# A chunked recurrence with two expert layers on one core: the first steps reordered

## The chip, the cores and the metric

One core of a Trainium2 chip runs one program. The metric is the device time of one execution in microseconds (us), as the median of three runs. TensorE, VectorE, ScalarE, GpSimd and SyncE (SP, which issues most transfers) run beside each other, each in the order of its own instructions.

## What is computed

The reference has three parts, in float32, each feeding the next. For 4 batches, 8 heads, 768 steps and a head dimension of 40:

```python
for t in range(S):
    y[:, :, t] = np.einsum('bhd,bhde->bhe', rt, state)
    Sa = np.einsum('bhde,bhe->bhd', state, at)
    state_decay = state * wt[:, :, None, :] - np.einsum('bhd,bhe->bhde', Sa, bt)
    state = state_decay + np.einsum('bhd,bhe->bhde', vt, kt)
```

The 3072 tokens of 320 numbers that come out pass a dense layer, `g = h * clip(h + 3, 0, 6) / 6` with `h = x @ w_in` (2048 wide) and `g @ w_out`; then a gate picks one of eight experts for each token, with `relu(x @ w1[e]) @ w2[e]`, 1024 wide, times the gate's weight.

## The kernel before

The recurrence is cut into 24 chunks of 32 steps (`C`, `NCH`), four chunks to a window of 128 steps (`SC`) and two chunks to a pair. Within a chunk the steps are solved at once: for each batch and head, N is a strictly lower 32x32 matrix of products between the scaled `a`, `k` and `b` of the chunk, and T its solved form. The path of one pair is: `turned` (TensorE transposes of the scaled rows, line 478, copied by line 483 into Z and KB), `gram_n` (the products L and N in one bank, line 506), `strict` (mask on VectorE, line 512), `keep` (L back into Z, line 517) and `store` (N to DRAM, `Nd`, line 523). `solve` loads N back from DRAM so that each partition holds one matrix (line 565), copies it twice (line 562), does 30 steps of two operations each (lines 574 and 575), and stores T (`Td`, line 583). `loads_t` (line 610) loads a chunk's T block by block into `Tb`, and `usolve` multiplies with it (u, line 649). The first pair is solved on VectorE, all later ones on GpSimd.

Window preparation (`window`, lines 385 to 453) makes decays from `w` by transposes and scans, and their reciprocals (`inv`, line 435). `scale` (line 439) multiplies the rows of `a`, `k` and `b` (`AKB`, tiles ra, rk, rb) with them. The prepared rows of each chunk go to DRAM in `Ed` and `KBd` by the window's function `keep(j)` (lines 441 to 451), and come back chunk by chunk (`loads_kb`, `loads_e`). `AKB` exists once, so a next window's rows may be loaded (`akb_rows`, line 1241: six transfers for one pair, line 358) only when the old ones are kept and transposed.

The code writes the order of every engine by hand (`tc.manual_schedule()`), and a scheduler adds the waits. Functions passed to `later(n, ...)` run n ticks on. Each transfer of SP or ScalarE holds one of eight completion semaphores (DMAHW0 to 7), and one that gets a semaphore already in use waits for it. The start (lines 1138 to 1284) prepares window 0, transposes and multiplies the first pair, starts `work0` (the first solve), and puts into it, at three of its steps (`S0, S1, S2`), the second pair's products with its solve (`next_gram`), and the first right-hand side followed by a burst of warmers (`before_solved`). Warmers are matmuls whose result nobody reads. `put0` stores T. Then the loop over chunks (line 1297) runs `rhs`, `usolve`, `usolve_cols`, `state`, `gram`, `turn_state`, `yout`, `cols_vr` for chunk c, the products of the pair four chunks ahead, the pieces of the next window and, from chunk 2 on, matmuls of the first dense layer (`dense`, `M.emit`, lines 263 and 304), which fill TensorE.

The dense layer's weights come as int64 pairs and are converted on VectorE (lines 116 to 118), split into two parts (lines 89 and 90), and for `w_out` turned on TensorE (line 158) and multiplied with the gate (line 169). There are 14 such units in a queue `wq`: six of `w_in` (three row blocks by two halves of the columns), then eight of `w_out`. `convert` says at which turn of which chunk how many are taken.

The first solve's own tile N0 lies in the buffer Z2, which the third pair needs as its Z; the loop's first chunk allocates it and GpSimd zeroes it (line 1382). `half_inverse(n)` (lines 1278 to 1284) takes the second window's reciprocals for half the heads and scales `rk` and `rb` with them.

## Time and profile before

| what | us |
|---|---|
| median of three runs | 1117.95 (1116.79 to 1120.19) |
| the profiled execution | 1113.57 |
| its span in the trace | 1111.8 |
| TensorE busy, share of the span | 1009.5, 91% |
| VectorE busy | 666.6, 60% |
| ScalarE busy | 650.1, 58% |
| GpSimd busy | 392.3, 35% |

Rows of a timeline have a start and a duration in us, the engine, the line, the operation, the tile written and the tiles read, the shape and a count; in brackets stands the idle time before it and what ended it. PE is TensorE, DVE VectorE, ACT ScalarE, POOL GpSimd; SPq is the issuing of transfers on SP. float32 matmuls stand in the trace as two instructions for one in the program.

### The profile page before, as it was taken

The numbers are of one execution on the slowest core, as the hardware profiler recorded it, in microseconds if no ns is written. First come the engines' busy times: TensorE is split into PE (matmuls) and PEld (weight loads), VectorE is DVE, ScalarE is ACT, GpSimd is POOL, SyncE is SP. The second block draws the span as 40 slices with busy tenths as digits, with TensorE's granted clock in tenths as the row PEclk, the third lists the DMA queues.
The fourth block names the chain that finished last, engine by engine and source line by source line (L and its number), as shares of the span: only waits on it lengthen the run. The fifth ranks groups of instructions, "written<-read, shape, count | busy, mean of one in ns | idle before, by whom it ended". The sixth has DMA issues, their size and how long they took to land. (4 is left out here: it accounts for less than half of the span.)

```text
span 1111.8 us, 36869 instructions
## 1 busy us (share of the span) xinstructions
PE 1009.5 (91%) x15540; PEld 944.4 (85%) x15540; DVE 666.6 (60%) x1338; ACT 650.1 (58%) x1370; POOL 392.3 (35%) x849
## 2 busy tenths in 40 slices
PE   4757799999999999998998999999999879999995
PEld 4756688888888888887887889999999779999995
DVE  7575447756546546543344455566557797787770
ACT  5324565777788778876677663433333545666551
POOL 5308345084575655846355401000000112332221
PEclk9578686999999999998998999999999989999998
DMA  9694966998798988989447532323333566766630
GB/s 135 126 151 73 165 128 104 128 183 137 135 175 141 159 141 156 159 139 192 95 93 144 111 90 78 100 82 97 104 106 112 191 186 208 220 208 197 209 90 16
DMA packets 362104, 151.82 MB, mean 137 GB/s; under 512 B 318663, under 2 KB 344775, under 8 KB 361932
## 3 DMA queue, kind: packets, MB, share of 16 engines
q1 hardware_dynamic: 352492, 129.45, 57.5%
q0 software_dynamic: 4992, 18.96, 6.0%
q8 instruction: 124, 2.03, 0.9%
q10 hardware_dynamic: 4448, 0.98, 0.5%
q14 instruction: 48, 0.39, 0.1%
HBM read 109.23 MB, written 40.12 MB: 134 GB/s over the span
## 5 line engine op out<-in xcount | busy, mean ns | idle before, releaser
L275 DVE SCALAR_TENSOR_TENSOR gf<-rl,h 128x512 f32<-128x512 f32 x96 | 65.6, 684 | 123.4 <-ACT rl L271 121.6
L263 PE MATMUL h<-xT,wi 128*128 128x256 f32 x768 | 119.9, 300 | 0.0
L280 DVE TENSOR_TENSOR gl<-gf,gh 128x512 fp32r<-128x512 f32 x78 | 55.4, 711 | 92.3 <-ACT gh L279 92.0
L271 ACT ACTIVATE rl<-h,half 128x512 f32<-128x512 f32 x96 | 65.9, 686 | 70.8 <-PE h L263 70.3
L263 PEld LDWEIGHTS h<-xT,wi 128*128 128x128 f32 x768 | 101.6, 196 | 3.4
L304 PE MATMUL x<-wo,gh 128*128 128x328 f32 x368 | 96.7, 348 | 0.5 <-ACT gh L279 0.5
L1703 POOL DMA_INDIRECT out_dram<-cyo,sidx x26 | 26.1, 1003 | 152.9 <-ACT cyo L1702 139.3
L279 ACT CAST gh<-gf 128x512 fp32r<-128x512 f32 x78 | 48.4, 620 | 38.4 <-DVE gf L275 37.9
L517 ACT COPY Z<-Ns 32x512 f32<-32x512 f32 x48 | 29.6, 618 | 64.4 <-DVE Ns L512 64.1
L304 PEld LDWEIGHTS x<-wo,gh 128*128 128x128 f32 x368 | 61.5, 197 | 5.0 <-ACT gh L279 0.7
L506 PE MATMUL LN<-Z,KB 104*64 104x32 f32 x1408 | 55.0, 235 | 9.0 <-POOL Z L1382 5.9
L1496 POOL DMA_DIRECT2D xTb<-xTd x10 | 5.4, 545 | 162.2 <-PE h L263 162.2
L506 PEld LDWEIGHTS LN<-Z,KB 104*64 104x64 f32 x1408 | 50.6, 152 | 14.0 <-POOL Z L1382 6.2
L483 ACT COPY KB<-t 40x512 f32<-40x512 f32 x86 | 49.8, 579 | 16.3 <-PE t L478 14.5
L304 PE MATMUL x<-wo,gl 128*128 128x328 f32 x184 | 59.1, 321 | 0.2 <-DVE gl L280 0.2
L717 PE MATMUL g<-YL,UV 104*64 104x32 f32 x1536 | 55.6, 227 | 0.0
L717 PEld LDWEIGHTS g<-YL,UV 104*64 104x64 f32 x1536 | 50.2, 141 | 5.7 <-issue 1.0
L1673 ACT ACTIVATE ghc<-ch 128x512 fp32r<-128x512 f32 x35 | 20.9, 598 | 51.0 <-PE ch L1667 50.0
L435 DVE RECIPROCAL It<-It 128x320 f32<-128x320 f32 (+1 forms) x20 | 50.3, 2531 | 0.1
L1587 POOL DMA_INDIRECT xg<-Xr,gidx x26 | 29.5, 1136 | 55.3 <-DVE sidx L1072 21.3
L724 DVE TENSOR_TENSOR YL<-g,mask 64x512 f32<-64x512 f32 x48 | 32.9, 685 | 20.3 <-PE g L717 19.9
L1096 PE MATMUL warm<-ident 128*128 128x128 f32 x258 | 44.5, 324 | 0.0
(787 smaller groups left out, 3057.1 us busy)
## 6 DMA issues: line engine op xcount, KB each, us to landing
raw<-in_moe_w_dram SPq DMA_DIRECT2D x26, 512.0 KB
raw<-in_moe_w_dram SPq DMA_DIRECT2D x26, 480.0 KB
xTd<-xT SPq DMA_DIRECT2D x12, 768.0 KB
xTb<-xTd POOLq DMA_DIRECT2D x10, 768.0 KB, 6.5
X<-KBd SPq DMA_DIRECT2D x46, 160.0 KB
raw<-in_moe_w_dram SPq DMA_DIRECT2D x13, 320.0 KB
xpd<-xpart SPq DMA_DIRECT2D x12, 328.0 KB
part<-xpd SPq DMA_DIRECT2D x12, 328.0 KB
```

What stands on the lines that cost most here:

```text
L263: nc.tensor.matmul(hp[:, i, :], lhsT=l, rhs=m, start=j == 0, stop=j == len(seq) - 1)
L271: nc.scalar.activation(v["t"], hv, AF.Relu, bias=half, scale=1.0 / 6.0)
L275: nc.vector.scalar_tensor_tensor(out=v["g"], in0=v["t"], scalar=1.0, in1=hv, op0=ALU.min, op1=ALU.mult)
L279: nc.scalar.copy(gh.rearrange("p i t -> p (i t)"), v["g"])
L280: nc.vector.tensor_tensor(out=gl.rearrange("p i t -> p (i t)"), in0=v["g"], in1=gh.rearrange("p i t -> p (i t)"), op=ALU.subtract)
L304: nc.tensor.matmul(st["x"][tt][:, :NX], lhsT=l[:, i, ts], rhs=W.wo[f][:, m, :], start=fp == 0 and i == 0 and j == 0, stop=fp == NFP - 1 an ...
L435: nc.vector.reciprocal(t, t)
L483: copy(dst[64:104, par::2].rearrange("p g b j t -> p g (b j) t"), pb[HP * par:HP * par + D].rearrange("p g b (j t) -> p g (b j) t", j=2))
L506: nc.tensor.matmul(pv[64 * q:64 * q + 64, g, bb, j, :], lhsT=KB[0:104, h, bb, j].rearrange("p x t -> p (x t)"), rhs=zh[0:104, h, bb, j, :] ...
L717: nc.tensor.matmul(pg[64 * q:64 * q + 64, g, bb, :], lhsT=uv[0:104, h, bb].rearrange("p x t -> p (x t)"), rhs=yl[0:104, h, bb, :], start=T ...
L724: nc.vector.tensor_tensor(out=yl[0:64, par::2], in0=pg[q:q + 64], in1=mask[q:q + 64, None, None, :].to_broadcast([64, 4, B, C]), op=ALU.mult)
L1096: nc.tensor.matmul(t[:, 0, 0:128], lhsT=ident, rhs=ident, start=True, stop=True)
```

## The change

- N is stored by matrix: `Nd` has the axis order h, b, j, i, t instead of i, h, b, j, t. A half's store is four transfers of 256 rows of 128 bytes instead of two of 64 rows of 1 KB; the load of a pair's N is two transfers of 64 rows of 4 KB instead of two of 2048 rows of 128 bytes.
- `keep(2)` and `keep(3)` of the first window go to SP instead of ScalarE, behind `akb_rows(0)`, which now follows `keep(1)`. `akb_rows(1)`, the fourth pair's rows, moves from `next_gram` behind u of chunk 0. Two weight loads (`WA.pull(2)`) move behind the loads of T.
- Z2 is allocated and zeroed, by ScalarE, right behind the store and load of T.
- VectorE scales only the third pair's rows (`pr0`); GpSimd scales the fourth pair's (`pr1`) behind yout of chunk 0. The second half of the reciprocals comes in two quarters, behind gram and behind yout of chunk 0.
- The units of the first weights are taken in another order, and by another `convert`.
- `keep_part` keeps one chunk a call over two chunks where it kept two.

```diff
-    Nd = dram.tile([NCH // 2, C, H, B, 2, C], F32, name="Nd")
+    Nd = dram.tile([NCH // 2, H, B, 2, C, C], F32, name="Nd")
...
+            if self.id == 0:
+                units = [units[n] for n in (0, 2, 4, 6, 7, 1, 8, 3, 5, *range(9, 14))]
...
-        def keep(j, eng=nc.sync):
+        def keep(j):
...
                 for par in range(2):
                     q = 64 * par
-                    nc.sync.dma_start(out=Nd[pr, :, 4 * half + par:4 * half + 4:2].rearrange("i g b j t -> i g (b j t)"), in_=Ns[q + 32:q + 64].rearrange("p (g x) -> p g x", g=2))
+                    for g in range(2):
+                        src = Ns[q + 32:q + 64].rearrange("p (g x t) -> p g x t", g=2, t=C)[:, g]
+                        nc.sync.dma_start(out=Nd[pr, 4 * half + 2 * g + par].rearrange("b j i t -> i (b j) t"), in_=src)
...
     keep(0)
     keep(1)
+    akb_rows(0)
+    keep(2)
+    keep(3)
     for i in range(3):
         now(U[2][i])
         now(U[3][i])
-    keep(2, nc.scalar)
-    keep(3, nc.scalar)
     some(4)
     now(wq, 1)
...
     def next_gram(hf):
-        if not hf:
-            akb_rows(0)
         now(U[2 + hf][3])
         flush_stores()
         if hf:
-            WA.pull(2)
-            akb_rows(1)
             solve(1, nc.gpsimd, None, nc.sync)()()
...
     loads_t(0)
+    Z.append(big.tile([128, H, B, 2, C], F32, tag="Z2", name="Z2"))
+    nc.scalar.copy(Z[2][0:64].rearrange("p h b j t -> p (h b j t)").rearrange("p (n x) -> p n x", x=128), zeros[0:64, None, :].to_broadcast([64, 2 * H, 128]))
     loads_e(0)
+    WA.pull(2)
...
-    scale(0, every)
+    scale(0, every, p=pr0)
...
-    def half_inverse(n):
-        hs = slice(n * H // 2, (n + 1) * H // 2)
+    def inverse(n, of):
+        hs = slice(n * H // of, (n + 1) * H // of)
         inv(every, hs)
         for i in range(1, 3):
-            scale(i, every, hs=hs)
-
-    half_inverse(0)
+            scale(i, every, p=pr0, hs=hs)
+
+    inverse(0, 2)
...
-    convert = {(0, 3): 2, (0, 5): 1, (0, 6): 1, (1, 1): 1, (1, 3): 2, (1, 4): 2, (1, 5): 1, (2, 2): 1, (2, 3): 1, (2, 4): 1}
+    convert = {(0, 6): 1, (1, 1): 1, (1, 2): 1, (1, 3): 1, (1, 4): 1, (1, 5): 1, (2, 1): 2, (2, 2): 1, (2, 4): 1, (2, 6): 1, (3, 1): 1, (3, 3): 1, (3, 5): 1}
...
-            Z.append(big.tile([128, H, B, 2, C], F32, tag="Z2", name="Z2"))
-            nc.gpsimd.memset(Z[2][0:64], 0.0)
...
         slot(usolve, c)
         if c == 0:
             loads_t(1)
+            akb_rows(1)
...
         slot(gram, c)
         if c == 0:
-            half_inverse(1)
+            inverse(2, 4)
...
         slot(yout, c)
+        if c == 0:
+            inverse(3, 4)
+            for i in range(3):
+                scale(i, every, nc.gpsimd, pr1)
```

How this moves the instructions stands in the order of each engine. On SP, round the first load of N (tile N_413 before, N_417 after), with the semaphores that it waits for. Before:

```order
L523 DMA Nd<-Ns_407 32x2x256 [waits DMAHW5_49,DVE_49]
L523 DMA Nd<-Ns_407 32x2x256 [waits DMAHW6_49]
L565 DMA N_413<-Nd 64x32x32 [waits DMAHW4_49,DMAHW5_49,DMAHW3_49,DMAHW6_49,DMAHW0_49,DVE_49]
L565 DMA N_413<-Nd 64x32x32 [waits DMAHW2_49]
```

With the change:

```order
L528 DMA Nd<-Ns_409 32x8x32 [waits DMAHW5_49,DVE_49]
L528 DMA Nd<-Ns_409 32x8x32 [waits DMAHW6_49]
L528 DMA Nd<-Ns_409 32x8x32 [waits DMAHW7_49]
L528 DMA Nd<-Ns_409 32x8x32 [waits DMAHW0_49]
L570 DMA N_417<-Nd 64x1024 [waits DMAHW4_49,DMAHW3_49,DMAHW5_49,DMAHW2_49,DMAHW6_49,DMAHW1_49,DMAHW7_49,DMAHW0_49,DVE_49]
L570 DMA N_417<-Nd 64x1024
```

Before, DMAHW0 and DMAHW2 are held by transfers that ScalarE issues; with the change all eight belong to the stores of N themselves.

Further on in SP's queue, from the rows of the next window to the loads of T (Tb). Before:

```order
L358 DMA rb<-in_b_dram 64x16x40 x2
L523 DMA Nd<-Ns_565 32x2x256 x2
L523 DMA Nd<-Ns_612 32x2x256 x2
L107 DMA wraw<-in_moe_w_in_dram 128x1024
L107 DMA wrawrv<-in_moe_w_in_dram 128x1024
L358 DMA ra<-in_a_dram 64x16x40 x2
L358 DMA rk<-in_k_dram 64x16x40 x2
L565 DMA N1None<-Nd 64x32x32 x2
L583 DMA Td<-N_413 1024x1x32 x2
L610 DMA Tb<-Td 32x8x32 x4
```

With the change:

```order
L361 DMA rb<-in_b_dram 64x16x40 x2
L447 DMA Ed<-Em 32x4x320
L452 DMA KBd<-rk 1024x1x40
L452 DMA KBd<-rb 1024x1x40
L528 DMA Nd<-Ns_569 32x8x32 x4
L528 DMA Nd<-Ns_618 32x8x32 x4
L570 DMA N1None<-Nd 64x1024 x2
L588 DMA Td<-N_417 1024x1x32 x2
L615 DMA Tb<-Td 32x8x32 x4
L107 DMA wraw<-in_moe_w_in_dram 64x1024
```

The weight loads and the second group of window rows (six transfers, of which the listing before leaves out the last two, rb) have gone from between the stores of N and the store of T, and two keeps of three transfers stand ahead of the stores (one is shown).

On VectorE, in chunk 0, from the mask of the gram (YL) to the low half of x (XS). Before:

```order
L724 TENSOR_TENSOR YL<-g_1018,mask 64x4x128 x2
L435 RECIPROCAL It_869<-It_869 128x4x160
L439 TENSOR_TENSOR rk<-rk,It_869 128x4x4x40
L439 TENSOR_TENSOR rb<-rb,It_869 128x4x4x40
L90 TENSOR_TENSOR wi_91<-wf_1004,wi_89 128x512
L90 TENSOR_TENSOR wi_92<-wf_1011,wi_90 128x512
L740 TENSOR_TENSOR x_1149<-y_1116,Et_861 128x320
```

With the change:

```order
L729 TENSOR_TENSOR YL<-g_1012,mask 64x4x128 x2
L438 RECIPROCAL It_873<-It_873 128x4x80
L442 TENSOR_TENSOR rk<-rk,It_873 64x4x2x40
L442 TENSOR_TENSOR rb<-rb,It_873 64x4x2x40
L745 TENSOR_TENSOR x_1134<-y_1101,Et_861 128x320
L438 RECIPROCAL It_873<-It_873 128x4x80
L442 TENSOR_TENSOR rk<-rk,It_873 64x4x2x40
L442 TENSOR_TENSOR rb<-rb,It_873 64x4x2x40
L752 TENSOR_TENSOR XS<-x_1134,XS 128x320
```

Two subtractions of the weights have left this place, and half of the reciprocals and products stands behind x. TensorE's list of chunk 0 has warmers of 4, 2 and 2 matmuls less: two ahead of and within the gram (line 717), one behind yout. On GpSimd the memset of Z behind the second solve's store of T is gone, and three products (ra, rk, rb, 64x32x40 each) stand there, ahead of the third solve.

## Rows read from the trace of the kernel before

**Rows 1.** The page: the span.

```profile
span 1111.8 us, 36869 instructions
```

**Rows 2.** Busy time by stretch: stretch, length, PE, PEld, DVE, ACT, POOL, PEclk, DMA, GB/s.

```profile
91.00:125.00 34.00, 24.83 (x457) 22.49 (x453) 15.74 (x20) 17.56 (x38) 26.11 (x56) 0.75 0.61 105
...
169.90:190.40 20.50, 20.50 (x250) 18.53 (x250) 16.32 (x30) 8.30 (x19) 12.40 (x28) 0.51 0.36 78
...
160.20:196.60 36.40, 35.40 (x542) 31.80 (x541) 24.02 (x40) 21.02 (x51) 20.61 (x47) 0.68 0.72 117
196.60:216.70 20.10, 19.06 (x490) 16.95 (x490) 16.10 (x24) 13.89 (x31) 0.00 (x0) 1.00 0.85 119
216.70:650.00 433.30, 411.62 (x9298) 366.32 (x9297) 224.12 (x347) 329.37 (x714) 241.44 (x594) 0.98 0.79 145
```

**Rows 3.** Timeline of VectorE round the first solve: start, duration, what.

```profile
44.49 0.69 DVE L118 SCALAR_TENSOR_TENSOR wf<-wraw,wf 128x512 int32<-128x512 int32 x1
...
53.01 0.19 DVE L574 TENSOR_TENSOR N<-N 128x30 f32<-128x30 f32 x1
...
71.27 0.22 DVE L578 MEMSET N<- 64x16 f32 x2
```

**Rows 4.** Waits of SP, 0 to 130 us: total, times, longest.

```profile
SPq L565 <- DMA Ed<-Em: 6.0, 1, 6.0
```

**Rows 5.** Timeline of SP's issuing: start, duration, transfers.

```profile
33.26 4.12 SPq L523 DMA_DIRECT2D Nd<-Ns  x4
44.30 2.92 SPq L565 DMA_DIRECT2D N<-Nd  x2
...
77.04 3.60 SPq L565 DMA_DIRECT2D N1None<-Nd  x2
80.74 2.82 SPq L583 DMA_DIRECT2D Td<-N  x2
86.32 1.83 SPq L610 DMA_DIRECT2D Tb<-Td  x4
...
145.64 2.51 SPq L565 DMA_DIRECT2D N2None<-Nd  x2
```

**Rows 6.** Timeline of TensorE: the burst of warmers, u, and grams of later pairs.

```profile
65.58 13.40 PE L1096 MATMUL warm<-ident 128*128 128x128 f32 x96
88.22 0.31 PE L649 MATMUL u<-rh,Tb 128*32 128x40 f32 x2 [9.24 <-DMA Tb<-Td]
...
89.85 1.27 PE L649 MATMUL u<-rh,Tb 128*32 128x40 f32 x58 [0.24 <-DMA Tb<-Td]
...
121.31 3.63 PE L506 MATMUL LN<-Z,KB 104*64 104x32 f32 x64 [5.93 <-POOL Z L1382]
...
206.57 2.04 PE L506 MATMUL LN<-Z,KB 104*64 104x32 f32 x64
```

**Rows 7.** Timeline of VectorE in chunk 0.

```profile
101.83 1.39 DVE L724 TENSOR_TENSOR YL<-g,mask 64x512 f32<-64x512 f32 x2 [12.36 <-PE g L717]
103.25 4.15 DVE L435 RECIPROCAL It<-It 128x640 f32<-128x640 f32 x1
...
110.84 0.49 DVE L740 TENSOR_TENSOR x<-y,Et 128x320 f32<-128x320 f32 x1
```

**Rows 8.** Timeline of GpSimd: a pair of products of the start, the third solve's first copy.

```profile
26.98 3.03 POOL L439 TENSOR_TENSOR ra<-ra,Em 64x640 f32<-64x640 f32 x2
...
150.31 0.60 POOL L562 COPY X2None<-N2None 64x512 f32<-64x512 f32 x1 [29.05 <-DMA N2None<-Nd]
```

**Rows 9.** PE and PEld by stretch: warmers (L1096), then w_out's transposes (L158) and products (L169).

```profile
91.00:125.00 34.00, 11.21 (x59) 9.11 (x59) 0.75 0.61 105
...
126.90:160.20 33.30, 2.75 (x15) 1.88 (x15) 0.91 0.68 138
...
126.90:160.20 33.30, 4.43 (x30) 4.09 (x30) 0.91 0.68 138
```

**Rows 10.** Groups of TensorE, 216 to 650 us: count, busy, mean ns, idle before and releasers.

```profile
L649 PE MATMUL u<-rh,Tb 128*32 128x40 f32 x1216 | 18.6, 214 | 4.9 <-DMA Tb<-Td 3.7 <-ACT rh L641 1.2
```

More of the change, by code (lines that the diff above doesn't have):

```diff
@@ L439, in scale @@
             (eng or nc.vector).tensor_tensor(out=t, in0=t, in1=(v["I"] if i else Em)[p, bs, hs], op=ALU.mult)
-        def keep(j, eng=nc.sync):
+        def keep(j):
             p, c = slice(C * j, C * j + C), SC * sc + j
-            eng.dma_start(out=Ed[c].rearrange("b t f -> t b f"), in_=Em[p].rearrange("p b h e -> p b (h e)"))
+            nc.sync.dma_start(out=Ed[c].rearrange("b t f -> t b f"), in_=Em[p].rearrange("p b h e -> p b (h e)"))
             for x in range(2):
@@ L448, in keep @@
                     continue
-                eng.dma_start(out=KBd[x, C * c:C * c + C].rearrange("t b (h e) -> t (b h) e", e=D), in_=AKB[1 + x][p, :, :, 0:D].rearrange("p b h e -> p (b h) e"))
+                nc.sync.dma_start(out=KBd[x, C * c:C * c + C].rearrange("t b (h e) -> t (b h) e", e=D), in_=AKB[1 + x][p, :, :, 0:D].rearrange("p b h e -> p (b h) e"))
             if j == 0 and sc < NSC - 1:
@@ L549, in solve @@
             tmp = p1.tile([128, 128], F32, tag="tmp", name=f"tmp{pr}{part}")
-        src, dst = Nd[pr].rearrange("i h b j t -> (h b) j i t"), Td[pr].rearrange("(g j) i t -> g j i t", j=2)
+        src, dst = Nd[pr].rearrange("h b j i t -> (h b) j i t"), Td[pr].rearrange("(g j) i t -> g j i t", j=2)
         if part is None:
-            src, dst = Nd[pr].rearrange("i h b j t -> (h b j) i t"), Td[pr]
+            src, dst = Nd[pr].rearrange("h b j i t -> (h b j) i t"), Td[pr]
         else:
@@ L1230, with akb_rows @@
     work0 = solve(0, nc.vector, None, nc.sync)
+    def akb_rows(j):
+        for n in range(6):
+            loads_akb(1, n // 2, j, n % 2)
     keep(0)
     keep(1)
+    akb_rows(0)
+    keep(2)
+    keep(3)
     for i in range(3):
@@ L1235 @@
         now(U[3][i])
-    keep(2, nc.scalar)
-    keep(3, nc.scalar)
     some(4)
     now(wq, 1)
-    def akb_rows(j):
-        for n in range(6):
-            loads_akb(1, n // 2, j, n % 2)
     def next_gram(hf):
-        if not hf:
-            akb_rows(0)
         now(U[2 + hf][3])
@@ L1364, in keep_part @@
         def keep_part(n):
-            if sc == 0 and j == 1:
-                for i in (2 * n, 2 * n + 1):
-                    win[1][-1](i)
+            if sc == 0 and j in (1, 2):
+                win[1][-1](2 * (j - 1) + n)
             elif j < 2 and 0 < sc < NSC - 1:
```

## The prediction

> **What bounds the kernel now.** I read four views, in this order. First the busy time by stretch, against the span [rows 1, 2]. From 216.7 to 650 us TensorE is busy 411.62 of 433.30 us at a clock share of 0.98: that stage is bound by TensorE, and whatever the first 200 us lose is carried whole to the end, because the later stages start from data and not at a time of day. The start is another matter: from 91 to 125 us TensorE is busy 24.83 of 34 us, 11.21 of these with warmers (59 matmuls that compute nothing) [rows 9], and the clock share of 0.75 says that it ran half of that stretch at the lower of its two levels (1.2 GHz, not 2.4). Every edit but the layout of N lies in this start, so the forecast is read from the start's chains.
>
> Second, the timeline of VectorE and the queue of SP round the first solve [rows 3 to 5]. The first solve needs N back from DRAM. The load is issued at 44.30 us although the stores' issue ended at 37.38. SP waited 6.0 us there, for an Ed transfer: one of the six that ScalarE issues for `keep(2)` and `keep(3)`. The order shows why: the load waits for DMAHW0, a completion semaphore that one of these holds. VectorE is through with other work at 45.2 (44.49 + 0.69), gets N only then, and solves from 53.01. The solve ends at 71.5, but the store of T is issued at 80.74: since N, SP has had to issue thirteen transfers of `keep` and `akb_rows(0)`, four stores, two weight loads, six transfers of `akb_rows(1)` and N of the second pair. T is loaded back from 86.32, and the first u ends at 91.1 (89.85 + 1.27) [rows 6].
>
> Third, the chunk that follows [rows 6, 7]. TensorE's gram of the third pair waits 5.93 us for a memset of Z2 on GpSimd, which stands behind the whole second solve, and ends at 124.94. VectorE, after the mask (ends at 103.22), takes a reciprocal of half the heads and four more operations before x at 110.84, for which the transposes on TensorE wait.
>
> Fourth, the wait of the steady stage [rows 10]: from 216 to 650 us u waits 3.7 us in all for T. There the change has little to win and something to lose.
>
> **The change, part by part.** The sum is made against the profiled execution, 1113.57 us with a span of 1111.8. The median of the timed runs, 1117.95, lies 4.4 above it, and I keep that distance.
>
> *First load of N.* With `keep(2)` and `keep(3)` on SP behind the load, nothing of ScalarE's stands ahead of it. Eight stores of 256 rows replace four of 64. Four loads of that very shape (T's, 32x8x32) issue in 1.83 us [rows 5], so the second half's stores, whose data is there at 36.6, are issued by 38.5 and land near 40. The load is then 64 rows of 4 KB a transfer instead of 2048 of 128 B. VectorE is busy until 45.2 anyway, so I put the copies there and the solve at 46.1: 6.9 us earlier, ending at 64.6. Bounds: nothing, if the small stores land as late as today's load is issued, and 6.9, since VectorE's other work is next.
>
> *Store of T and u.* `akb_rows(1)` and two weight loads leave the queue ahead of T; six transfers of `keep` and four stores come in, and N and N1 shrink from 8192 rows to 256. From N's load at 44.30 to T's store at 80.74 about 25,000 small rows passed: twelve window transfers and eight of `keep` at 1024 rows, and N's 4096. That is 690 a us. Six window transfers and eight of `keep` are 14,300, or 21 us: from 42 to 63. The stores and N1's load add about 2, and I take T's issue at 66.5, 2 us behind the solve, where today it is 9.2. From T's issue to the end of u is 10.4 us today with N1's 4096 rows in front; with 128 I take 9. So u ends near 75.5, **15.6 us** earlier with the first term. Bounds: T issued as the solve ends (17.6), or as long after N's load as today, 36.4 us, at 76.4 (5.7).
>
> *Chunk 0.* Today 33.8 us pass from the end of u to the end of the gram. The order takes 8 warmers out, 16 matmuls in the trace at 0.19 us (11.21 over 59), 3.0 us, of which 12, 2.2 us, lie ahead of the mask. Of the reciprocal of half the heads, 4.15, a quarter is half, 2.1, and a product of that width is as wide as x, 0.49 [rows 7]. So, in today's frame: mask ends at 101.0, reciprocal and two products at 104.1, x at 104.6, the second quarter at 107.7, the low half of x at 108.2, its transposes at 108.8, a warmer, then the gram from 109.5 to 111.6, at the 2.04 us that it takes at full clock [rows 6]. Z2's zeros are now a ScalarE copy that waits for T's store alone and lies beside T's way back. That is **13 us**. Bounds: 5.9, if only the memset's wait goes, and 15, if the clock stays up through u as well: the burst of warmers that ends at 78.98, 9 us ahead of u, now ends at its heels.
>
> *Fourth pair.* Its six loads follow u and lie beside chunk 0. Its three products go from VectorE to GpSimd behind the second solve, about 3 us each by a pair of half-width ones of the start [rows 8]. That solve starts with N1, some 16 us earlier, and the third solve waits 29.05 us for its N [rows 8], so they are covered; without that cover the third pair's T would come 9 us later.
>
> *Weights by use.* The conversions stay fourteen, but they move back. A w_out block costs TensorE (2.75 + 4.43)/5 = 1.44 us [rows 9]. Chunk 1 has two fewer: **-3**. Behind u of chunk 3 stand two more, 2.9 on TensorE, and on VectorE some 4.6 (two conversions at 1.3 and the subtractions behind them), which has 16.10 of 20.1 us taken there [rows 2]. Both are then full; I take **+3.5**. Chunk 2's share of VectorE, 24.02 of 36.4 us, has room.
>
> *Stores in the steady stage.* Two more issues a chunk, 0.45 each, stand ahead of the loads of T, against a load of N every second chunk that needs 2.5 us to issue today [rows 5] and then has 64 rows a transfer. I take **+2** (-3 to +8). T's own store is 2048 rows of 128 B; it and N1's 4096 landed within 9.3 us of the first issue, 77.04 to 86.32, so 1024 such rows cost 1.6 us at most.
>
> Here the Trainium skill speaks against the change: *DMA: Bandwidth & Descriptors*, Specifications, gives 512 B as the least transfer at line rate, with a read-modify-write below, and the new stores write 128 B where the old wrote 1 KB. By that rule the last rival below would be the likely one; no row here shows a small write's own duration.
>
> Sum: -15.6 - 13 - 3 + 3.5 + 2 = -26, less 2 for waits that I don't see: 1117.95 - 24 = **1094 us**.
>
> **The rivals.** *The queue stays full.* If T's store comes 36.4 us behind N's load as today, T's term shrinks by 9.9: 1104. For it: six transfers move into this stretch, and the stores double. Against: N's and N1's small rows are gone. *VectorE holds chunks 2 and 3.* The reciprocals of the next window meet eight conversions there instead of three; each chunk could lose 4 us more: 1102. *The clock recovers early.* From 169.9 to 190.4 TensorE runs at the lower level though it is busy throughout [rows 2]; no row shows a cause that the change takes away, so I leave it. If the smoother start keeps the clock up, chunk 2 is bound by VectorE's 24 us plus some 5 of conversions, near 30 and not 36.4: 1088. *Slower: the small stores hold T.* If a half's stores land as late as the 2048 rows of N2's load do (issued at 145.64, copied at 150.31, 4.7 us [rows 5, 8]), T comes some 4 us later in the 20 halves of the steady stage. u waits for T in some chunks already, so if half of that is lost, it is 2 x 20 = 40: 1134. It outweighs the gain from 24/20 = 1.2 us a chunk on. Against it stands T's own store. That an edit doesn't do what it says has little room: the order shows each move.
>
> **The numbers.** Forecast 0.62, queue full 0.13, VectorE full 0.10, clock 0.09, slow stores 0.06. The range, 1081 to 1108, takes in the first four with the bounds of T's term (+10, -2), chunk 0 (+7, -2), the steady stage and the clock. A measurement of this kernel tells about 0.3% (3.4 us) from no change. Faster by more 0.92, within it 0.03 (slow stores near their turning point), slower 0.05.
>
> **What would show it.** Right: N's load issued near 40 and the solve at 46; T's store within 3 us of the solve's end; u ending near 75; no wait of the gram for Z, and the gram's end near 96; w_out blocks fewer in chunk 1 and more in chunk 3; everything from chunk 5 on 22 to 28 us earlier, with chunks as long as today. Wrong: T's store waiting in SP's queue, VectorE without idle time in chunks 2 and 3, or u waiting for T in most chunks.

## The result, and the profile after

| | before | with the change |
|---|---|---|
| median of four runs, us | 1117.37 (1115.79 to 1120.19) | 1129.15 (1128.29 to 1135.16) |
| ratio to before, 95% interval | | 1.012 [1.0086, 1.0155] |
| span of the profiled execution, us | 1111.8 | 1126.8 |
| chunk 0 (u of chunk 0 to u of chunk 1) | 38.7 | 25.1 |
| chunk 1 | 33.4 | 42.9 |
| chunk 2 | 36.4 | 34.6 |
| chunk 3 | 20.1 | 42.2 |
| chunks 5 to 22 | 412.3 | 421.9 |
| u of chunk 23 to the end | 458.8 | 461.9 |

The change makes the kernel 1.2% slower; the forecast was 24 us faster. The lengths are read from the starts of the u rows of each profile, and say where the time went: the first u comes 13.0 us earlier (75.25 for 88.22 in [rows 6]) and chunk 0 gives another 13.6, together 26.5 where 28.6 was forecast. Chunks 1 and 3 then lose 9.5 and 22.1, and the steady stage 9.6.

First the start. Timeline of SP's issuing (start, duration, transfers), to hold against [rows 5]:

```profile
31.41 6.10 SPq L528 DMA_DIRECT2D Nd<-Ns  x8
38.79 1.13 SPq L570 DMA_DIRECT2D N<-Nd  x2
...
59.83 6.13 SPq L528 DMA_DIRECT2D Nd<-Ns  x8
67.40 1.14 SPq L570 DMA_DIRECT2D N1None<-Nd  x2
68.58 1.31 SPq L588 DMA_DIRECT2D Td<-N  x2
73.36 1.94 SPq L615 DMA_DIRECT2D Tb<-Td  x4
```

The wait for Ed is gone and N's load is issued at 38.79, not 44.30. The stores take 6.1 us of issue where they took 4.1 at the same place [rows 5], and the second eight stand ahead of N1 and T. VectorE's timeline, the first and the last row of the solve [rows 3]:

```profile
44.25 1.29 DVE L579 TENSOR_TENSOR N<-N 128x30 f32<-128x30 f32 x1
...
63.62 0.22 DVE L583 MEMSET N<- 64x16 f32 x2
```

The solve ends 7.7 us earlier, T is issued 12.2 us earlier, 4.7 behind the solve and not 9.2. TensorE's timeline, to hold against [rows 6]: u of chunk 0, the gram of the third pair, then in chunk 1 the gate products of a w_out block (8 columns wide) and a half of g, and in chunk 3 a w_out block's transposes:

```profile
75.25 0.31 PE L654 MATMUL u<-rh,Tb 128*32 128x40 f32 x2 [4.66 <-DMA Tb<-Td]
...
97.25 2.06 PE L509 MATMUL LN<-Z,KB 104*64 104x32 f32 x64
...
108.35 0.93 PE L169 MATMUL wg<-wg,wtT 128*128 128x8 f32 x6 [0.64 <-ACT wtT L162]
...
112.02 1.92 PE L722 MATMUL g<-YL,UV 104*64 104x32 f32 x32
...
185.95 0.90 PE L158 MATMUL wt<-ident,wf 128*128 128x128 f32 x3 [6.18 <-DVE wf L118]
```

The gram no longer waits for Z. But half of g takes 1.92 us in chunk 1, and TensorE stands idle for 6.18 us in chunk 3. The same half of g in the kernel before:

```profile
134.93 1.12 PE L717 MATMUL g<-YL,UV 104*64 104x32 f32 x32
```

Busy time by stretch (columns as in [rows 2]): chunks 1, 2 and 3, the steady stage at the length of [rows 2], then two pieces of chunks 1 and 3:

```profile
100.30:143.20 42.90, 40.74 (x562) 36.38 (x561) 24.78 (x36) 21.63 (x51) 21.80 (x31) 0.68 0.66 136
143.20:177.90 34.70, 29.15 (x546) 25.58 (x546) 27.73 (x44) 22.14 (x51) 20.99 (x46) 0.90 0.74 129
177.90:220.00 42.10, 34.76 (x509) 30.68 (x508) 21.89 (x37) 15.90 (x40) 4.30 (x6) 0.59 0.60 93
220.00:653.30 433.30, 405.14 (x9136) 360.47 (x9134) 216.59 (x334) 323.56 (x695) 236.21 (x589) 0.97 0.78 140
...
109.30:133.20 23.90, 23.90 (x267) 21.72 (x265) 12.40 (x19) 7.38 (x19) 4.81 (x2) 0.50 0.52 114
184.40:218.50 34.10, 31.40 (x423) 27.80 (x424) 17.99 (x31) 15.27 (x37) 2.96 (x4) 0.50 0.51 83
```

From 109.3 to 133.2 and from 184.4 to 218.5 the granted clock is 0.50, the lower level (1.2 GHz), though TensorE is busy 23.90 of 23.90 and 31.40 of 34.10 us. Chunk 3 had a share of 1.00 before [rows 2]. So a wait of 0.64 us stands ahead of 24 us at half speed, and one of 6.18 ahead of 34.

Who is late in chunk 3 is read on VectorE and SP, then in chunk 1 on GpSimd and VectorE (timelines):

```profile
177.34 1.10 SPq L107 DMA_DIRECT2D wrawrv<-in_moe_w_out_dram  x1
...
184.51 0.33 DVE L116 TENSOR_SCALAR wf<-wrawrv 128x320 int32<-128x320 int32 x1 [4.22 <-DMA wrawrv<-in_moe_w_out_dram]
...
107.70 3.32 POOL L442 TENSOR_TENSOR rk<-rk,It 64x1280 f32<-64x1280 f32 x1
110.98 3.13 POOL L442 TENSOR_TENSOR rb<-rb,It 64x1280 f32<-64x1280 f32 x1
...
108.31 3.06 DVE L90 TENSOR_TENSOR wo<-wf,wo 128x320 fp32r<-128x320 f32 x1
111.37 2.92 DVE L116 TENSOR_SCALAR wf<-wrawxT 128x320 int32<-128x320 int32 x1
```

The thirteenth weight unit's raw words are asked for at 177.34, behind six transfers of window rows (170.59 to 177.22), and VectorE waits for them until 184.51. In chunk 1 VectorE's operations end just behind GpSimd's products: a subtraction that takes 0.48 us later in the chunk takes 3.06.

The steady stage is told by the u group (TensorE, 220 to 653 us) against [rows 10]: the wait for T grows from 3.7 to 5.9, and the clock share falls from 0.98 to 0.97.

```profile
L654 PE MATMUL u<-rh,Tb 128*32 128x40 f32 x1216 | 19.3, 218 | 7.8 <-DMA Tb<-Td 5.9 <-ACT rh L646 1.7
```

### The profile page after: what moved, and what is told of

It reads as the page before. It is cut to its first block, busy times and chain, and to the rows that moved or that the text cites. A ratio compares the mean times of both kernels' runs of the same rounds, so it can differ in the third digit from the quotient of the medians.

```text
span 1126.8 us, 36918 instructions
## 1 busy us (share of the span) xinstructions
PE 1023.8 (91%) x15528; PEld 955.9 (85%) x15528; DVE 676.5 (60%) x1341; ACT 654.1 (58%) x1371; POOL 398.8 (35%) x851
## 5 line engine op out<-in xcount | busy, mean ns | idle before, releaser
L729 DVE TENSOR_TENSOR YL<-g,mask 64x512 f32<-64x512 f32 x48 | 32.9, 685 | 25.0 <-PE g L722 24.6
```

Of the source, the lines that this page charges most:

```text
L729: nc.vector.tensor_tensor(out=yl[0:64, par::2], in0=pg[q:q + 64], in1=mask[q:q + 64, None, None, :].to_broadcast([64, 4, B, C]), op=ALU.mult)
```

## The experiments

All runs in one table; the ratio is against the kernel before, measured beside each group of runs. Chunk lengths are of one profiled execution each. The same program differs from one execution to the next by up to 25 us in these versions, so small differences between single profiles are not read.

| run | first u | chunk 0 | 1 | 2 | 3 | 5 to 22 | median us (range, runs) | ratio |
|---|---|---|---|---|---|---|---|---|
| e1_raw_first | 77.2 | 24.2 | 42.2 | 35.9 | 30.9 | 421.7 | 1122.3 (1117.7–1129.2, 10) | 1.004 [1.001, 1.007] |
| e2_old_weights | 77.8 | 32.9 | 37.3 | 32.5 | 22.9 | 421.8 | 1115.0 (1109.3–1127.4, 10) | 0.998 [0.994, 1.002] |
| e3_old_nd | 76.1 | 24.1 | 43.0 | 36.6 | 38.9 | 415.2 | 1116.7 (1106.7–1120.3, 10) | 0.996 [0.992, 1.000] |
| e4_vector_scale | 77.1 | 32.6 | 42.6 | 36.4 | 39.8 | 429.0 | 1133.4 (1121.2–1145.7, 10) | 1.011 [1.007, 1.015] |
| e5_swap | 77.4 | 24.5 | 31.9 | 38.1 | 41.0 | 423.3 | 1122.4 (1111.4–1127.9, 10) | 1.002 [0.998, 1.005] |
| e6_start_only | 75.8 | 33.2 | 46.3 | 35.8 | 20.5 | 411.4 | 1108.8 (1104.7–1111.2, 4) | 0.989 [0.984, 0.995] |
| e7_nd_only | 90.2 | 39.2 | 35.4 | 36.6 | 20.1 | 421.3 | 1134.0 (1123.9–1140.5, 10) | 1.013 [1.010, 1.016] |
| e8_combo | 75.3 | 24.3 | 33.4 | 38.5 | 38.8 | 416.2 | 1111.0 (1103.8–1112.4, 8) | 0.991 [0.988, 0.994] |
| e9_products | 76.3 | 33.3 | 37.1 | 36.1 | 20.5 | 411.4 | 1105.3 (1101.6–1106.8, 4) | 0.991 [0.987, 0.994] |
| e10_spread | 75.6 | 23.8 | 35.8 | 45.4 | 21.6 | 413.2 | 1102.1 (1096.4–1102.8, 4) | 0.986 [0.981, 0.990] |
| e11_four_big | 91.0 | 38.8 | 35.1 | 35.7 | 20.5 | 428.8 | 1138.1 (1136.1–1139.8, 4) | 1.019 [1.015, 1.023] |
| e12_t_first | 89.3 | 39.2 | 33.1 | 36.5 | 20.0 | 429.8 | 1136.2 (1134.6–1140.2, 4) | 1.018 [1.014, 1.023] |
| e13_spread_t | 75.6 | 24.6 | 33.0 | 45.5 | 31.4 | 425.1 | 1114.0 (1104.9–1122.3, 12) | 0.996 [0.993, 0.999] |

### The parts undone one at a time

**e1_raw_first**, the changed kernel with one load moved:

```diff
         if c == 2:
+            if pulled[0] < 14 and raws[pulled[0] + 1] <= laid[0]:
+                pulled[0] += 1
+                WA.pull(1)
             for i in range(3):
                 next_akb(i, True)
```

> The changed kernel with one transfer moved: the raw words of the thirteenth weight unit are asked for ahead of the six window rows (ra, rk, rb) of chunk 2, and not behind them. Late weights: in the changed kernel that load was issued at 177.34 us behind six transfers, VectorE waited for it until 184.51, TensorE stood idle for 6.18 us and then ran at the lower clock from 184.4 to 218.5. If that one load is the cause, TensorE has no wait over 1 us in chunk 3, the clock stays up, chunk 3 (u to u) takes 20 to 24 us and not 42.2, and the time is 1107 to 1112 us, that is 17 to 22 below the changed kernel. Rival, the clock: if the stretch at the lower clock would come there anyway, as it came to chunk 2 of the kernel before, only the 6 us of the wait come back: 1122 to 1124. Rival, VectorE full: the wait goes to another conversion, chunk 3 stays over 35 us, 1126 to 1131.

Chunk 3 fell from 42.2 to 30.9 and the 6.18 us of idle time are gone, so that load was the cause of the wait. The time fell by 7 us, into the range of the clock rival, and not by 17 to 22: a wait of 0.81 us is left, for the next unit, with the lower clock behind it (195.4 to 209.1), and another such stretch (171.6 to 185.2) reaches in from chunk 2.

TensorE's timeline in chunk 3 of this run:

```profile
193.89 0.55 PE L158 MATMUL wt<-ident,wf 128*128 128x128 f32 x3 [0.81 <-DVE wf L118]
```

Busy time of its chunk 3 (the clock share is the last number but two):

```profile
179.50:210.30 30.80, 29.50 (x509) 26.38 (x508) 19.82 (x35) 15.79 (x39) 3.67 (x6) 0.69 0.78 117
```

**e2_old_weights**:

```diff
-            if self.id == 0:
-
-                units = [units[n] for n in (0, 2, 4, 6, 7, 1, 8, 3, 5, *range(9, 14))]
...
-    convert = {(0, 6): 1, (1, 1): 1, (1, 2): 1, (1, 3): 1, (1, 4): 1, (1, 5): 1, (2, 1): 2, (2, 2): 1, (2, 4): 1, (2, 6): 1, (3, 1): 1, (3, 3): 1, (3, 5): 1}
+    convert = {(0, 3): 2, (0, 5): 1, (0, 6): 1, (1, 1): 1, (1, 3): 2, (1, 4): 2, (1, 5): 1, (2, 2): 1, (2, 3): 1, (2, 4): 1}
```

> The changed kernel with the order of the weight units and the table of their conversions as before. Late weights: only three conversions are left for chunk 2 and none for chunk 3, so chunk 3 takes some 20 us again (42.2 in the changed kernel), and the 17 us by which u of chunk 2 led are kept from there on, less the 10 that the steady stage loses: 1105 to 1112 us. If the six conversions in chunk 1 meet GpSimd's products there, chunk 1 grows past its 42.9 us, and the time is nearer 1112. Rival, the start itself: if the clock, and not the weights, sets chunks 1 to 3, they last as long as in the changed kernel together (119.7 us), and the time is 1126 to 1132.

Chunk 3 is back at 22.9 and the median 14 us below the changed kernel, 3 us short of what late weights expected; chunk 0 pays, 32.9 for 25.1, as three conversions are back there and TensorE waits 3.99 us behind them, ahead of the gram.

**e3_old_nd**, with the load of N back in the same way:

```diff
-    Nd = dram.tile([NCH // 2, H, B, 2, C, C], F32, name="Nd")
+    Nd = dram.tile([NCH // 2, C, H, B, 2, C], F32, name="Nd")
...
-                    for g in range(2):
-                        src = Ns[q + 32:q + 64].rearrange("p (g x t) -> p g x t", g=2, t=C)[:, g]
-                        nc.sync.dma_start(out=Nd[pr, 4 * half + 2 * g + par].rearrange("b j i t -> i (b j) t"), in_=src)
+                    nc.sync.dma_start(out=Nd[pr, :, 4 * half + par:4 * half + 4:2].rearrange("i g b j t -> i g (b j t)"), in_=Ns[q + 32:q + 64].rearrange("p (g x) -> p g x", g=2))
```

> The changed kernel with N stored as before: two transfers of 64 rows of 1 KB for each half, loaded in rows of 128 bytes. Small stores: from u of chunk 5 to u of chunk 23 the changed kernel takes 421.9 us and the kernel before 412.3; if the four stores of 128-byte rows ahead of T's load cost that, it falls to about 412, and the start gives back 3 to 6 us of its gain by the slower load of N: 1121 to 1125 us. Rival, the order of issue alone: the steady stage keeps its 420 us or more, for another reason (the clock, another transfer ahead of T), and the time is 1129 to 1135.

The steady stage fell from 421.9 to 415.2 and the time by 12 us, more than expected, because the start gives nothing back: first u at 76.1 and chunk 0 of 24.1. So the quicker load of N in the start was not the layout's doing. With the old layout it is issued at 39.15, and with the new layout alone (e7) at 50.30, later than before; what brings it forward is that no transfer of ScalarE stands ahead of it, the one whose semaphore it waited for [rows 4]. SP's issuing in e3:

```profile
33.47 4.12 SPq L526 DMA_DIRECT2D Nd<-Ns  x4
39.15 1.82 SPq L568 DMA_DIRECT2D N<-Nd  x2
```

**e4_vector_scale**:

```diff
-                scale(i, every, nc.gpsimd, pr1)
+                scale(i, every, nc.vector, pr1)
```

> The changed kernel with the fourth pair's three products on VectorE, at the same place in the program, and not on GpSimd. Engines that hold each other up: in the changed kernel GpSimd's products last from 104.83 to 114.1 us, and in just that time three operations of VectorE take 3.24, 3.06 and 2.92 us, where the same forms take 0.4 to 0.8 elsewhere. If that sets the 42.9 us of chunk 1, chunk 1 takes 33 to 36 us, and the time is 1119 to 1123. Rival, the clock: chunk 1 is long because TensorE runs at the lower clock from 109.3 to 133.2, whatever VectorE does; chunk 1 takes over 40 us and the time stays within 4 us of the changed kernel. Rival, the other side: VectorE, which has no idle time from 87 to 104 us, takes three products more there and waits for the rows of b: up to 6 us slower.

Missed. Chunk 1 keeps its 42.6 us without GpSimd's products, and the ratio (1.011) is that of the changed kernel (1.012), as the clock rival has it; so the products were not what made chunk 1 long there. The profile is of the longest of ten executions and would not carry this alone, but e5 agrees: there the products stay on GpSimd, two operations of VectorE beside them take 3.01 and 3.07 us, and chunk 1 takes 31.9. Chunk 0 lost 7.5 us in this profile, with the three products on VectorE, which is the third theory's place.

**e5_swap**:

```diff
-                units = [units[n] for n in (0, 2, 4, 6, 7, 1, 8, 3, 5, *range(9, 14))]
+                units = [units[n] for n in (0, 2, 4, 1, 6, 7, 8, 3, 5, *range(9, 14))]
```

> The changed kernel with one pair of units exchanged in the order of the weights: chunk 1 takes the sixth block of w_in behind its u, and w_out blocks only behind its gram. In the changed kernel and in three of the runs so far, a w_out block stands between s and g of chunk 1; TensorE waits 0.63 us for it, has eight products of 8 columns there where twelve warmers stood, and the lower clock begins right behind it (109.3 to 133.2 us in the changed kernel). With the old order of the weights there was no such block, and the clock held through g. The place of the block: chunk 1 then takes 33 to 37 us and not 42.9, and the time is 1119 to 1123 us against 1129. Rival, the clock falls anyway: the start's warmers and GpSimd's products bring it down with any weights; chunk 1 stays over 41 us, and the time within 4 us of 1129. Rival, VectorE: the block of w_in is wider (512 columns to 320), so chunk 1 loses what it gains, 1126 to 1130.

Chunk 1 takes 31.9 us, 11 less, at a clock share of 0.95 (0.68 with the change), and the median is 6.8 lower: the place of the w_out block was the cause. Chunk 1 takes 42.2 to 43.0 us in the four profiles with the block there (the changed kernel, e1, e3, e4) and 31.9 to 35.8 in the four whose new order has none there (e5, e8, e10, e13). Whether the block acts by the wait of 0.64 us or by its thin products in the place of warmers is not separated. The stall of chunk 3 is still there, 2.92 us with 34.1 us at the lower clock behind it. Busy time of its chunk 1:

```profile
101.90:133.80 31.90, 30.28 (x567) 27.09 (x569) 22.99 (x34) 20.90 (x50) 16.55 (x19) 0.95 0.80 166
```

### The start alone, the layout alone

**e6_start_only** has both diffs, that of e2 and that of e3.

> The changed kernel with the weights' order and conversions as before and N stored as before, so the new start alone. Weights gave 14 us and the store of N 12 when undone one at a time. If they are separate causes, both together give 24 to 28: 1102 to 1106 us, faster than the kernel before. Rival, they overlap (both act by T and the weights standing in one queue, or by the lower clock, which takes back what is won): 1108 to 1114. Rival, the start itself gives nothing: 1117 to 1120.

The two parts undone together give 20 us and not 24 to 28, and the time lies in the range of the overlap rival. The new start alone is faster than the kernel before, by 1.1%, but keeps only 9 of the 18 us by which its second u leads (108.95 for 126.87): chunk 1 takes 13 back. Timelines of TensorE, ScalarE, VectorE and GpSimd there, and then busy time of the stretch that follows:

```profile
119.09 1.09 PE L478 MATMUL t<-ident,rb 64*104 64x64 f32 x8 [3.87 <-ACT UV L464]
...
117.21 0.62 ACT L89 CAST wi<-wf 64x512 fp32r<-64x512 f32 x1 [4.65 <-DVE wf L118]
...
113.91 3.27 DVE L118 SCALAR_TENSOR_TENSOR wf<-wrawrv,wf 64x512 int32<-64x512 int32 x1
...
113.29 3.35 POOL L439 TENSOR_TENSOR rb<-rb,It 64x1280 f32<-64x1280 f32 x1
```

```profile
118.40:145.70 27.30, 26.61 (x279) 24.20 (x280) 9.40 (x22) 10.08 (x25) 1.29 (x3) 0.50 0.51 104
```

The timelines read from the bottom up: VectorE's operation does not end before GpSimd's product, the cast on ScalarE waits for that, the copy of UV stands behind the cast, TensorE waits 3.87 us, and the clock is at its lower level from 118.4, within that wait, to 145.7. That VectorE stands still beside such a product is what the Trainium skill states (*SBUF — State Buffer*, Who interferes with whom: an operation of VectorE with two inputs in SBUF contends with one of GpSimd that reads SBUF, over a pair of ports that is an exclusive lock); the rows agree, 3.27 us beside 3.35, where this operation takes 0.68 in the kernel before. The unit's three operations take 2.91, 3.26 and 3.27 us here (the 2.37 that the next expectation gives is a row of e2).

It is the meeting in time that costs. In e2 the same three products begin 2.9 us later (110.34 for 107.40) and hold only the last of this unit's operations. The copy of UV begins at 114.82 and not at 117.86, TensorE does not wait ahead of g, and chunk 1 takes 37.3 us.

**e9_products** takes those products away from that place:

```diff
             inverse(3, 4)
-            for i in range(3):
-                scale(i, every, nc.gpsimd, pr1)
+        if c == 1:
+            for i in range(3):
+                scale(i, every, nc.vector, pr1)
```

> The kernel with the new start alone (weights and N's store as before), with the fourth pair's three products on VectorE behind yout of chunk 1, and not on GpSimd behind yout of chunk 0. In the run of the new start alone, chunk 0 gave 38.7 to 33.2 us and chunk 1 took it back, 46.3 us for 33.4: TensorE waited 3.87 us for a ScalarE copy (UV) that stood behind a ScalarE cast, which stood behind one of three VectorE operations that took 3.27, 2.37 and 2.91 us beside GpSimd's products, and the lower clock began there (118.4 to 145.7). GpSimd's products as the cause: without them at that place the wait goes, the clock holds through g and LN, chunk 1 takes 33 to 37 us, and the time is 1096 to 1101 against 1108.8. Rival, the clock comes down in chunk 1 anyway: chunk 1 over 42 us, the time 1105 to 1111. Rival, VectorE: the products there delay xT or the conversions of chunk 2, which loses what chunk 1 wins: 1104 to 1112.

Chunk 1 fell from 46.3 to 37.1 and no wait is left ahead of its gram. Busy time of chunk 1 (the clock share was 0.68 in e6):

```profile
109.60:146.70 37.10, 34.88 (x580) 31.75 (x579) 20.80 (x40) 21.29 (x56) 10.91 (x24) 0.82 0.69 144
```

The median is 3.5 us lower, which is the rivals' range and not the theory's, and the two ratios do not differ (0.991 and 0.989, with intervals that overlap). The cause of the wait is shown, by this run and by e2; that the wait made chunk 1 long rests on one profile of each; a gain over e6 is not shown.

**e7_nd_only** is the kernel before with e3's diff turned round, the layout of `Nd` alone.

> The kernel before with nothing but N's layout of the change: four stores of 128-byte rows for each half, loads of 64 rows of 4 KB. Small stores: the steady stage (u of chunk 5 to u of chunk 23) grows from 412.3 us by 5 to 9, and the start wins at most 2 by the quicker load of N: 1122 to 1128 against 1118 or 1119. Rival, only together: the stores cost time only where the change made the queue late, and the time stays within 3 us of the kernel before.

Slower by 16 us, more than any theory gave: 9 in the steady stage, 4 in chunks 1 and 4, 2 in the start.

**e11_four_big** asks which property of the new stores does it:

```diff
-                    nc.sync.dma_start(out=Nd[pr, :, 4 * half + par:4 * half + 4:2].rearrange("i g b j t -> i g (b j t)"), in_=Ns[q + 32:q + 64].rearrange("p (g x) -> p g x", g=2))
+                    for g in range(2):
+                        nc.sync.dma_start(out=Nd[pr, :, 4 * half + 2 * g + par].rearrange("i b j t -> i (b j t)"), in_=Ns[q + 32:q + 64].rearrange("p (g x) -> p g x", g=2)[:, g])
```

> The kernel before with its own layout of N (rows of 1 KB), but each store cut into two: four stores of 32 rows for each half, where the layout of the change has four of 256 rows of 128 bytes. That layout alone made the kernel before 15.9 us slower (1134.0 against 1118.1). Number of issues: each further issue takes 0.45 us on SP's queue, up to 1.4 where the queue is full, ahead of T's load, and in quiet stretches a store of 128-byte rows lands 1.4 to 1.7 us after its issue, no later than one of 1 KB rows (1.5 to 1.7); so this run is as slow as that one: 1128 to 1136, steady stage (u of chunk 5 to u of chunk 23) 418 to 423 us. Rival, the size of the rows (the Trainium skill, DMA: Bandwidth & Descriptors, Specifications, has rows below 512 B at less than line rate): rows of 1 KB cost nothing more, 1116 to 1121, steady stage 412 to 414. Both in part: 1122 to 1127.

Four stores of 1 KB rows cost as much as four of 128-byte rows, and more. So it is not the size of the rows that costs: two more transfers a half cost as much with rows of 1 KB. The u groups of TensorE, 220 to 654 us, of e7 and then of e11:

```profile
L651 PE MATMUL u<-rh,Tb 128*32 128x40 f32 x1216 | 20.6, 218 | 9.9 <-DMA Tb<-Td 7.3 <-ACT rh L643 1.7 <-ACT rl L271 0.4
```

```profile
L650 PE MATMUL u<-rh,Tb 128*32 128x40 f32 x1152 | 21.3, 225 | 12.4 <-DMA Tb<-Td 10.7 <-ACT rh L642 1.1
```

SP's queue ahead of T in one chunk, again of e7 and then of e11:

```profile
334.90 3.29 SPq L525 DMA_DIRECT2D Nd<-Ns  x4
338.23 1.97 SPq L612 DMA_DIRECT2D Tb<-Td  x4
```

```profile
339.17 3.28 SPq L524 DMA_DIRECT2D Nd<-Ns  x4
342.49 1.90 SPq L611 DMA_DIRECT2D Tb<-Td  x4
```

Four issues take 3.3 us here whatever their rows; over the stage they take 1.8 to 3.4 us (e7) and 1.7 to 3.5 (e11), where two took 0.8 to 1.4 before. That e11 is the slower of the two may come from its old load of N (1.9 to 2.6 us of issue for 1.1 to 2.1); no run tests it. u waits 7.3 and 10.7 us for T where it waited 3.7 [rows 10]. The rest is the clock: its share from 216 to 650 us is 0.96 and 0.95, for 0.98 [rows 2]. Busy time of that stretch in e7:

```profile
216.00:650.00 434.00, 405.54 (x9053) 360.07 (x9052) 221.69 (x338) 322.62 (x696) 239.69 (x594) 0.96 0.79 141
```

By the rounded shares 0.02 of 434 us is 8.7; with 3.6 of waiting that is an estimate of 12, where the stage lost 9.0.

**e12_t_first** is e7 with T's load ahead of the stores in chunks 4 to 18, and **e13_spread_t** the same move in e10, below:

```diff
+        if SC <= c < NCH - LEAD - 1:
+            loads_t(c + 1)
         flush_stores()
...
-        if more and c and c != NCH - LEAD - 1:
+        if more and c and c != NCH - LEAD - 1 and not SC <= c < NCH - LEAD - 1:
             loads_t(c + 1)
```

> The kernel before with the change's layout of N alone (1134.0 us, where the kernel before stands at 1118.1), and with one more edit: in chunks 4 to 18 the load of the next chunk's T is issued ahead of the stores of N, and not behind them. The place in the queue: if the four stores cost by standing ahead of T's load, u no longer waits for T, the steady stage (u of chunk 5 to u of chunk 23) falls from 421.4 us to 410 or 413, and the time to 1120 to 1125 (the start's 2 to 4 us stay). Rival, the number of transfers as such: the two more transfers of each half fill SP's queue for everything behind, N's load and the next chunk's rows among it, wherever T stands; the steady stage stays over 418 and the time over 1129. Rival, T not ready: the load now waits for GpSimd's solve of that pair and holds the stores and rows behind it: 1134 to 1150.

> The quickest version so far (new start, N stored as before, one weight unit at each turn of chunks 1 and 2: 1102.1 us) with T's load ahead of the two stores of N in chunks 4 to 18. The place in the queue: u waits for T in some of these chunks even with two stores (3.7 us in the kernel before), and each wait can bring the lower clock; without them 2 to 5 us go: 1097 to 1100. Rival, nothing left to win: 1100 to 1103. Rival, T not ready: the load waits for the solve and holds what is behind it, 1104 to 1112.

e12 is no faster than e7 (1136.2 for 1134.0, with intervals that overlap), and e13 loses 12 us to e10. SP's queue stands where the third theory has it, since T is not solved and stored yet. SP's waits in e12, 220 to 654 us (total, times, longest):

```profile
SPq L612 <- DMA Td<-X7None: 5.4, 1, 5.4
SPq L612 <- DMA Td<-X5None: 5.1, 1, 5.1
SPq L612 <- DMA Td<-X3None: 5.0, 1, 5.0
```

With three shorter ones these come to 22.5 us, and e7 has none of them. u's own wait for T fell to 2.0 us, but N's stores and the rows behind stood still meanwhile. e12's time and steady stage (429.8) lie in the second theory's range too, and 10 of the 19 us between the profiles of e13 and e10 stand in chunk 3, ahead of the edit. So T's load gains nothing at the earlier place, and whether the issues cost by their place ahead of T or by filling the queue is not settled.

### Versions that beat both kernels

**e8_combo**: the diffs of e3 and e5, and a second request for raw words, behind a turn's conversions:

```diff
                 laid[0] += 1
+            while c > 1 and pulled[0] < 14 and raws[pulled[0] + 1] <= laid[0]:
+                pulled[0] += 1
+                WA.pull(1)
```

> The changed kernel with N stored as before, the units exchanged as in the run on the place of the block, and from chunk 2 on each weight block's raw words asked for as soon as their buffer is free. If the three causes are separate (late weights 7 to 20, the block in chunk 1 6 to 10, the stores 8 to 12): chunk 1 takes 33 to 37 us, chunk 3 20 to 24, the steady stage 412 to 415, and the time is 1095 to 1103 us. Rival, the clock takes it back: where TensorE has less to wait for, another stretch at the lower clock appears; chunks 1 to 3 together stay over 105 us (89.9 in the kernel before, 119.7 in the changed one), and the time is 1106 to 1115.

The rival took it: 1111.0. Chunk 3 takes 38.8 us with raw words in time; TensorE waits 1.87 us for a conversion that stands behind a reciprocal on VectorE, and from 175.9 to 210.0 the clock is at 0.50. Timeline of TensorE there, and busy time of that stretch:

```profile
175.31 0.55 PE L158 MATMUL wt<-ident,wf 128*128 128x128 f32 x3 [1.87 <-DVE wf L118]
```

```profile
175.90:210.00 34.10, 32.65 (x432) 29.29 (x433) 18.24 (x30) 15.57 (x38) 4.11 (x8) 0.50 0.67 86
```

**e10_spread**: e8 with another order and table.

```diff
-                units = [units[n] for n in (0, 2, 4, 1, 6, 7, 8, 3, 5, *range(9, 14))]
+                units = [units[n] for n in (0, 2, 4, 1, 6, 3, 7, 5, *range(8, 14))]
...
+    convert = {(0, 6): 1, **{(1, n): 1 for n in range(1, 7)}, **{(2, n): 1 for n in range(1, 7)}}
```

> The changed kernel with N stored as before and the weights spread in another way: one unit at each of the six turns of chunk 1 and of chunk 2, none in chunk 3, w_in blocks ahead of w_out blocks in chunk 1, raw words asked for as soon as their buffer is free. In the combined run chunk 3 took 38.8 us though no raw words were late by much: TensorE waited 1.87 us for a w_out block behind VectorE's reciprocals and the lower clock followed (175.9 to 210.0). Weights in chunk 3 as the cause: without a unit there chunk 3 takes 20 to 24 us, chunks 0 and 1 some 25 and 33, and the time is 1092 to 1100. Rival, VectorE in chunk 2: two more units beside the reciprocals and the next window's scans make chunk 2 wait, 40 to 48 us, and the time 1102 to 1110. Rival, the clock: a stretch of 20 us or more at the lower clock comes in chunks 2 and 3 whatever stands there, 1108 to 1114.

The quickest: 0.986 of before, and 0.974 of the changed kernel (0.9856/1.012). Its interval overlaps those of e8 and e9. The time is the first rival's, and so is chunk 2 with 45.4 us; chunk 3 takes 21.6 without a weight unit, as the cause has it, but 31.4 in e13, whose program differs only from chunk 4 on.

## Why the prediction was wrong

*First load of N, T and u, chunk 0* (-28.6 in all): right in the main. N's load came at 38.79 (near 40), the solve ended at 63.8 (64.6), u began its last 62 matmuls at 76.3 and ended near 78 (75.5), the gram ended at 99.3 (near 96) with no wait for Z. Measured at the second u it is 26.5. Two reasons were wrong. The layout had no part in N's early load (e3). And T's store came 4.7 us behind the solve, not 2: the window transfers were through by 59.8, sooner than the 63 of the forecast, but the eight stores and N1's load, put at "about 2", took 8.7 us (59.83 to 68.54).

*"Whatever the first 200 us lose is carried whole to the end."* From chunk 5 on it held: e6, the start alone, leads by 6.1 us at u of chunk 5 and by 7.0 at u of chunk 23. Ahead of that it failed for gains: e6 leads by 18 us at the second u and by 5 at the third. A lead survives only if the chunks behind it keep their clock, and the sum carried chunks 1 to 4 at the clock that they had in the profile of before. The lower level was set aside ("no row shows a cause that the change takes away"), though a change can also add a cause.

*Weights by use* (-3 and +3.5): failed by size. Chunk 1 lost 9.5 and chunk 3 22.1. I priced each unit as busy time on TensorE and VectorE, 1.44 and 2.3 us. What it costs is a wait on TensorE if the unit is late, behind raw words in SP's queue (e1), behind reciprocals on VectorE (e8), or with thin products where warmers stood (e5), and then 14 to 34 us at half clock. The rival "VectorE holds chunks 2 and 3" named chunk 3 but not the cause: VectorE is busy for 21.89 of 42.1 us there and waits for raw words itself, and chunk 2 became shorter. Undoing the weights alone gave 14 us (e2), and 8 where N was stored as before (e3 to e6, 1116.7 to 1108.8).

*Stores in the steady stage* (+2, from -3 to +8): failed by size. The stage grew by 9.6 us in the changed kernel and by 9.0 with the layout alone (e7), and the whole kernel by 12 (e3) and 16 (e7). The two issues a chunk that I counted at 0.45 us each take 1.0 to 2.0 together, the wait for T rises, and the rest of the loss is the clock. The last rival gave 1134 and the right sign for a wrong reason: it priced small rows landing late, and by the Trainium skill (*DMA: Bandwidth & Descriptors*, Specifications) rows below 512 B move at less than line rate. No run shows that here: where the four issues follow each other without a pause, the last part of a store lands 1.5 to 1.7 us after its issue both with rows of 128 bytes (e7) and with rows of 1 KB (e11), at 32 KB a store, and e11 settles that the time is not lost by the rows.

Put together by the ratios: the start -1.1% (e6), the weights +0.7% (e3 against e6), the stores +1.6% (changed kernel against e3), in all +1.2%. The split depends on the order: undone the other way round, the weights are +1.4% (changed kernel against e2) and the stores +0.9% (e2 against e6), so the two parts overlap.

## What to carry to other kernels

Where an engine's clock has two levels, a new wait on it can cost many times its length. Before such a change, list which waits of a microsecond its order can create, give the stretch at the lower level a price and a chance of its own in the sum, and let several executions tell whether it comes: here not every such wait was followed by one. Count issues and not only bytes on a queue that a critical load shares, and look at what the busiest queue holds just ahead of it. Undo a bundle's parts one at a time and together: here a start worth 1% was hidden under two edits that cost more.

## What was not expected of the hardware

- A short wait of TensorE was followed by a long stretch at the lower clock, in which it was busy nearly throughout (23.90 of 23.90 us from 109.3 to 133.2). The stretch does not follow the wait in length: 0.64 us stood ahead of 23.9, 0.81 ahead of 13.7 (e1, 195.4 to 209.1), 1.87 ahead of 34.1, 3.87 ahead of 27.3, 6.18 ahead of 34.1. And not every such wait has one behind it. Of the other waits for a w_out block in chunks 1 and 2 of the changed kernel's own profile, take two: behind the first, of 0.54 us, the lower level lasted 3.4 us (140.0 to 143.4), and behind the second, of 1.27, the share stayed at 1.00 until 163.9 (TensorE's timeline):

```profile
138.08 0.93 PE L169 MATMUL wg<-wg,wtT 128*128 128x8 f32 x6 [0.54 <-ACT wtT L162]
...
150.28 0.81 PE L169 MATMUL wg<-wg,wtT 128*128 128x8 f32 x5 [1.27 <-ACT wtT L162]
```

- One program can take either course. e13's is that of e10 up to chunk 4, and its last wait of over 1 us ahead of chunk 3 was as long (3.27 us, for 3.38 in e10). The lower level began within 0.6 us of its end in both, and lasted 41.0 us in e13 and 17.1 in e10. So one execution does not tell whether the clock falls, or for how long, and why a stretch ends when it does stays open. Busy time of chunk 3 in e10 and then in e13:

```profile
180.60:202.20 21.60, 21.24 (x491) 19.09 (x490) 13.35 (x21) 13.37 (x31) 0.00 (x0) 0.87 0.58 89
```

```profile
178.70:210.10 31.40, 31.40 (x491) 28.57 (x490) 15.54 (x24) 13.61 (x31) 2.38 (x3) 0.52 0.47 73
```

- Stores of 128-byte rows were no slower to land than stores of 1 KB rows, and cutting a store in two without changing its rows cost 1.9% of the kernel [1.5, 2.3].
- From the last chunk's u to the end every version took 460.9 to 463.5 us, the kernel before 458.8 in its one profile; no run tells why.
